# Second product of the experts on plain float32 operands, in a one-core kernel of attention, experts and a gated linear unit

## The chip, the core and the metric

The program runs on one core of one Trainium2 chip. The metric is the device time of one execution in microseconds (us); the time before is the median of three runs. TensorE (PE in the profile) does the matrix products, with its weight loads in a row of their own (PEld); VectorE is DVE, ScalarE is ACT, GpSimd is POOL, SyncE is SP and issues most transfers. The profile is one execution recorded by the hardware.

## The reference

Three layers follow each other over 3072 tokens of 512 numbers: banded attention, a mixture of experts, and a gated linear unit.

```python
x = attn_out.transpose(0, 2, 1, 3).reshape(B * S, H * D)     # 3072 x 512
x = _moe_ref(x=x, **moe_kwargs)
return _moe2_ref(x=x, **moe2_kwargs)
# _moe_ref: do_compute = x @ w_skip > 0; e_idx = argmax(x[do_compute] @ w_gate)
for e in range(E):                                           # E = 8
    mask = e_idx == e
    h = np.maximum(xc[mask] @ w1[e], 0.0)                    # 512 -> 1024
    y[mask] = gate_w[mask, None] * (h @ w2[e])               # 1024 -> 512
out[do_compute] = xc + y
# _moe2_ref: gate = 1/(1+exp(-(x @ w_gate))); (gate * (x @ w_val)) @ w_out, 512 -> 1536 -> 512
```

The weights of the gated linear unit arrive as float64 and are converted on the chip.

## The kernel before

The attention comes first (to about 290 us), then the experts (to about 556 us), then the gated linear unit. Most products are made in three parts: each operand is split into a high part of type float32r (ScalarE copies it, which rounds) and a low part, the difference (VectorE or GpSimd subtracts), and TensorE adds up high times high, high times low and low times high. A few products run on plain float32 operands: probabilities times values in the attention (L413, L414, 65 columns wide). Transposes (L443, L762) take plain float32 too.

The experts' weights come in chunks of 512 KB, numbered n: for expert e, 8e to 8e+3 are w1 and 8e+4 to 8e+7 are w2. `load_chunk` brings a chunk into a ring of six raw buffers; `split_chunk` makes the two parts (L733 on ScalarE, L735 on VectorE or GpSimd). GpSimd takes the low parts of the chunks with n % 8 in (0, 2, 6) and of the first ones, VectorE the others. Expert 0 is done as two tiles of 128 tokens ("0a", "0b") by `expert_tile`, in the wait for the routing of the last batch; experts 1 to 7 are done by `expert`, each with 256 places for tokens; a further tile of 128 tokens ("overflow", e = 8), which runs with these inputs, is done by `expert_tile` at the end.

In `expert` the first product (L779) has 96 matmuls of 256 columns; its result is relu'd and split into `hT` (L783, L784). The second product (L801) has 16 products of 512 columns, three matmuls each. `hook1` follows each quarter of the first product and `hook2` each quarter of the second; between them they put into the queues, in program order, the splits of the next expert's chunks, the transposes of the next expert's tokens (L762, L765, L766), the gather of the tokens of the expert after that (L748) and the steps of `convert` for the gated linear unit's weights: words loaded into `cvw` by SP (L1173), squares on ScalarE (L1182), L1195, L1196, L1199 and then L1201, L1202 on VectorE, and an addition on GpSimd (L1203). Each engine works through its queue in that order. SP's queue holds the chunk loads and the `cvw` loads in program order as well, and a load whose buffer is still in use holds up those behind it.

Of the kernel before, what the change touches and what calls it, by code (L numbers as in the profile page):

```python
# [63 lines left out]
def attention_moe_glu_kernel(  # L64
# [14 lines left out]
    # ------------------------------------------------------------------ constants  # L79
# [40 lines left out]
    # expert weights: quads of four [128, 1024] chunks, w1(0), w2(0), w1(1), ...  # L120
# [14 lines left out]
    def load_chunk(n, after=None):  # L135
        t = (raw_p if n % 6 > 3 else rawb[0]).tile([P, 1024], F32, tag="raw", name=f"raw{n}")
        src = chunk_src(n)
        if after is not None:
            after.memset(t[:, 0:1], 0.0)
        nc.sync.dma_start(t if (n % 8) < 4 else t.rearrange("p (a f) -> p a f", a=2), src)  # L140
        raw_q[n] = t

    chunks = {}
    general = []

    # ------------------------------------------------------------------ attention
    with ExitStack() as actx:
# [14 lines left out]
        # distances, and a large number for what is masked: the scores of head h are taken times 2^(h+1), the  # L162
        # reciprocal of its slope
# [31 lines left out]
        def prime_v(G):  # L195
            """value blocks 1..4 with the first keys, the global ones, in place of their own first rows"""
# [25 lines left out]
        def k_task(G, pr, c):  # L222
            """key transposes of blocks 2c, 2c+1 of a pair of heads, each stacked twice"""
# [88 lines left out]
        def prep_tasks(G):  # L312
            """(early part, late part)"""
# [33 lines left out]
        def emit_global(n):  # L347
            """the first keys, the global ones, in place of the first of the block"""
# [173 lines left out]
        # bias tiles from the run-time n_local and n_global  # L522
# [34 lines left out]
        # products of no use while the loads are under way: the array's clock goes up with its load  # L557
# [6 lines left out]
        def busy(n):  # L564
            # the same through the waits of the last logits
# [150 lines left out]
    # ------------------------------------------------------------------ experts  # L716
    with ExitStack() as ectx:
# [922 lines left out]
```

## Time and profile before

| what | value |
|---|---|
| median of three runs | 1160.47 us (1160.18 to 1168.36) |
| profiled execution: its time, the span from first to last instruction | 1162.3 us |
| TensorE busy in the span | 1080.8 us (93%) |
| VectorE, ScalarE, GpSimd busy | 775.5, 529.4, 345.7 us |
| mean granted TensorE clock | 0.960 |

The page lists one execution; its span is all the time that it gives, and it lies 1.8 us over the median. Busy shares are means over stages with different limits, so the stages have to be read apart: the page cuts the span into 40 slices, and VectorE's digits are 7 to 9 up to slice 20 and 3 or 4 from slice 25 on, where TensorE's are all 9.

### The profile page before, as it was taken

The page shows a single profiled execution, that of the slowest core. Times are in us where ns is not written, and L with a number is a line of the kernel's source. Part 1 is how long each engine was busy: PE and PEld are TensorE (multiplying, and loading weights), DVE is VectorE, ACT ScalarE, POOL GpSimd, SP SyncE. Part 2 cuts the span into 40 slices and gives each one's busy share as a digit, 9 for nine tenths or more (in the row PEclk, how much of TensorE's full clock was granted, in tenths as well). Part 3 has the DMA queues.
Part 4 walks back from the last instruction along what each step waited for, and adds up shares of the span by engine and source line. Part 5 has one row for each costly group of instructions (what it writes and reads, how often), then busy time and mean ns, then how long its engine had stood idle before and what let it go on. Part 6 is the DMA issues. An engine that isn't in the chain of part 4 may idle for free.

```text
span 1162.3 us, 16223 instructions
## 1 busy us (share of the span) xinstructions
PE 1080.8 (93%) x5870; PEld 927.1 (80%) x5870; DVE 775.5 (67%) x1584; ACT 529.4 (46%) x929; POOL 345.7 (30%) x349
## 2 busy tenths in 40 slices
PE   6899899898888888888999999999999999999998
PEld 6788888887677777776787888888888888888886
DVE  6899879797679999998788734443444343444342
ACT  5787666665334444445444433333433333333232
POOL 3786565673546556554222100000000000000000
PEclk7999888899899988889999999999999999999999
DMA  8355455252457777765332110020010002001000
GB/s 164 100 146 137 102 124 132 65 148 80 150 188 252 237 234 231 232 229 171 100 109 73 37 55 1 1 73 1 1 60 14 1 1 73 1 1 37 1 1 36
DMA packets 104106, 110.23 MB, mean 95 GB/s; under 512 B 55888, under 2 KB 82256, under 8 KB 103632
## 3 DMA queue, kind: packets, MB, share of 16 engines
q1 hardware_dynamic: 101296, 100.18, 29.3%
q0 software_dynamic: 2720, 8.92, 2.1%
q8 instruction: 49, 0.80, 0.3%
q14 instruction: 41, 0.34, 0.1%
HBM read 86.27 MB, written 17.30 MB: 89 GB/s over the span
## 4 chain that ended last, share of the span: by engine, by line
PE 48%; DVE 3%; issue 0%; ACT 0%; DVEq 0%
PE gv L1080 32%; PE o L1100 16%; PE gx L1046 1%; DVE wgvs L1057 0%; DVE wgv L1196 0%; DVE wo L1199 0%; DVE wo L1196 0%; DVE gt L1088 0%; DVE gm L1086 0%; ACT gt L1087 0%; DVE cvbo L1202 0%; DVE wos L1064 0%; DVE gxl L1040 0%; DVE cvbo L1201 0%; PE gx L1035 0%
## 5 line engine op out<-in xcount | busy, mean ns | idle before, releaser
L1080 PE MATMUL gv<-gxh,wgvs 128*128 128x512 f32 x1152 | 367.7, 391 | 1.7 <-ACT gxh L1039 1.0
L1080 PEld LDWEIGHTS gv<-gxh,wgvs 128*128 128x128 f32 x1152 | 216.1, 188 | 46.9 <-ACT gxh L1039 1.2
L1080 PE MATMUL gv<-gxl,wgvs 128*128 128x512 f32 x576 | 223.4, 389 | 0.3 <-DVE gxl L1040 0.3
L1100 PE MATMUL o<-wos,gt 128*128 128x512 f32 x864 | 207.6, 389 | 0.0
L1086 DVE TENSOR_TENSOR gm<-gv,sg 128x512 f32<-128x512 f32 x72 | 49.7, 690 | 221.4 <-PE gv L1080 221.4
L1100 PEld LDWEIGHTS o<-wos,gt 128*128 128x128 f32 x864 | 162.1, 188 | 33.9 <-DVE wos L1064 0.3
L1087 ACT ACTIVATE gt<-gm 128x512 fp32r<-128x512 f32 x72 | 45.5, 632 | 216.2 <-DVE gm L1086 216.2
L1080 PEld LDWEIGHTS gv<-gxl,wgvs 128*128 128x128 f32 x576 | 108.2, 188 | 22.6 <-DVE gxl L1040 0.7
L779 PE MATMUL h<-xeh,we 128*128 128x256 f32 x448 | 93.6, 308 | 24.2 <-POOL we L735 18.0
L376 ACT ACTIVATE p<-t,mn 128x256 f32<-128x256 f32 (+1 forms) x192 | 83.3, 482 | 63.8 <-DVE mn L367 63.5
L1085 ACT ACTIVATE sg<-gv 128x512 f32<-128x512 f32 x72 | 43.0, 598 | 135.1 <-PE gv L1080 122.1
L779 PEld LDWEIGHTS h<-xeh,we 128*128 128x128 f32 x448 | 78.4, 213 | 27.2 <-POOL we L735 19.0
L1057 DVE TENSOR_TENSOR wgvs<-wgv,wgvs 128x1024 fp32r<-128x1024 f32 x72 | 91.0, 1264 | 11.1 <-ACT wgvs L1056 10.9
L1088 DVE TENSOR_TENSOR gt<-gm,gt 128x512 fp32r<-128x512 f32 x72 | 49.9, 693 | 50.2 <-ACT gt L1087 50.2
L801 PE MATMUL y<-we,hT 128*128 128x512 f32 x336 | 81.8, 395 | 1.7 <-DVE we L735 1.7
L342 PE MATMUL s<-ks,qs 128*128 128x256 f32 (+1 forms) x384 | 72.8, 313 | 9.3 <-DVE ks L352 5.1
L367 DVE CUSTOM_DVE_ANT_0 t<-s,far 128x256 f32<-128x256 f32 (+1 forms) x192 | 68.7, 394 | 15.1 <-PE s L342 14.6
L1056 ACT ACTIVATE wgvs<-wgv 128x1024 fp32r<-128x1024 f32 x72 | 75.5, 1049 | 0.4 <-ACTq L1558 0.4
L735 POOL TENSOR_TENSOR we<-raw,we 128x1024 fp32r<-128x1024 f32 (+1 forms) x27 | 67.9, 2522 | 25.6 <-ACT we L733 13.5
L733 ACT ACTIVATE we<-raw 128x1024 fp32r<-128x1024 f32 x68 | 70.6, 1052 | 9.7 <-DMA raw<-in_moe_w_dram 6.2
L414 PE MATMUL o<-v,pts 128*128 128x65 f32 x384 | 73.3, 284 | 0.4 <-PE pt L385 0.4
L801 PEld LDWEIGHTS y<-we,hT 128*128 128x128 f32 x336 | 61.5, 188 | 14.2 <-DVE we L735 2.1
(268 smaller groups left out, 1856.8 us busy)
## 6 DMA issues: line engine op xcount, KB each, us to landing
raw<-in_moe_w_dram SPq DMA_DIRECT2D x68, 512.0 KB, 4.1
qraw<-in_q_dram SPq DMA_DIRECT2D x16, 384.0 KB, 3.6
kraw<-in_k_dram SPq DMA_DIRECT2D x32, 192.0 KB, 4.0
v<-in_v_dram SPq DMA_DIRECT2D x8, 768.0 KB, 5.6
x_rows<-x SPq DMA_DIRECT2D x48, 128.0 KB, 2.4
cvwg<-in_moe_w_gate_dram SPq DMA_DIRECT2D x12, 512.0 KB, 4.9
cvwg<-in_moe_w_val_dram SPq DMA_DIRECT2D x12, 512.0 KB, 4.9
cvwo<-in_moe_w_out_dram SPq DMA_DIRECT2D x12, 512.0 KB, 3.5
```

The costliest lines, as they stand in the source:

```text
L342: nc.tensor.matmul(st[:, a, c0:256], qt[:, a, i * P:(i + 1) * P], kt[:, a, e, k0:(i + 1) * P], start=(e == 0), stop=(e == 1))
L367: nc.vector.tensor_tensor_reduce(o, i0, i1, 2.0 ** -(h0 + a + 1), 3.0e38, ALU.add, ALU.min, mn[:, a:a + 1])
L376: nc.scalar.activation(p[:, a, c0:], t[:, a, c0:], AF.Exp, bias=mn[:, a:a + 1], scale=-1.0)
L414: nc.tensor.matmul(o[:, hh, :], t[:, a, 1, :], vt[:, hh, i, :], start=(i == 0), stop=True)
L733: nc.scalar.activation(t[:, 0, :], r, AF.Copy)
L735: low = lambda sl: eng.tensor_tensor(t[:, 1, sl], r[:, sl], t[:, 0, sl].bitcast(F32), ALU.subtract)
L779: nc.tensor.matmul(ph[:, a, :n], chunks[cb + c][:, wl, m * P:(m + 1) * P], xx[:, c, :n], start=(s_ == 0), stop=(s_ == len(seq) - 1))
L801: nc.tensor.matmul(ys[u], hh[:, hl, f % 2, u * P:(u + 1) * P], w[:, wl, (f % 2) * DM:(f % 2 + 1) * DM], start=(f == 0 and s_ == 0), stop=( ...
L1056: nc.scalar.activation(t[:, 0], wgv[m], AF.Copy)
L1057: nc.vector.tensor_tensor(t[:, 1], wgv[m], t[:, 0].bitcast(F32), ALU.subtract)
L1080: nc.tensor.matmul(pt, w[:, wl, c, gv, :], xx[:, c, :], start=(i == 0), stop=(i == len(seq) - 1))
L1100: nc.tensor.matmul(ops[g][u], gt[:, hl, u * P:(u + 1) * P], w[:, wl, :], start=(m == 0 and i == 0), stop=(m == NM - 1 and i == 2))
```

## The change

The second product of every expert takes plain float32 operands: the relu'd first product is kept once as float32, and the w2 chunks are used as they are loaded, so that one matmul instruction stands where three stood. The low part of `hT` and both parts of the w2 chunks are no longer made. The w1 chunks are still split, all their low parts now on VectorE. The w2 chunks have eight buffers of their own ("web", of 4 KB per partition where four of 8 KB were); the ring of six raw buffers holds w1 chunks, and chunks 4 and 5 at the start. Loads go out as buffers come free by count (`free`, `loads`) and not by the count of splits. The four splits per expert are all issued from `hook2`.

```diff
     def load_chunk(n, after=None):
-        t = (raw_p if n % 6 > 3 else rawb[0]).tile([P, 1024], F32, tag="raw", name=f"raw{n}")
+        if n % 8 > 3:
+            pool, tag = (raw_p, "raw") if n < 6 else (web[0], "web")
+        else:
+            pool, tag = (raw_p if ring_place(n) > 3 else rawb[0]), "raw"
+        t = pool.tile([P, 1024], F32, tag=tag, name=f"raw{n}")
...
-        web = ectx.enter_context(tc.tile_pool(name="web", bufs=4))
+        web.append(ectx.enter_context(tc.tile_pool(name="web", bufs=8)))
...
-        def split_chunk(n, late=None):
-            pool, tag = (wea, "wea") if n % 8 < 4 else (web, "web")
-            t = pool.tile([P, 2, 1024], F32R, tag=tag, name=f"we{n}")
+        def split_chunk(n):
+            t = wea.tile([P, 2, 1024], F32R, tag="wea", name=f"we{n}")
             r = raw_q.pop(n)
             nc.scalar.activation(t[:, 0, :], r, AF.Copy)
-            eng = nc.gpsimd if n < 6 or n == 9 or n % 8 in (0, 2, 6) and n < 8 * NE + 1 else nc.vector
...
+            nc.vector.tensor_tensor(t[:, 1, :], r, t[:, 0, :].bitcast(F32), ALU.subtract)
...
-                hh = hp.tile([P, 2, 2, 2 * P], F32R, tag="h", name=f"hT{key}_{mp}")
-                nc.scalar.activation(hh[:, 0, :, :n], ph[:, :, :n], AF.Relu)
-                nc.vector.scalar_tensor_tensor(
-                    hh[:, 1, :, :n], ph[:, :, :n], 0.0, hh[:, 0, :, :n].bitcast(F32), ALU.max, ALU.subtract)
+                hh = hp.tile([P, 2, 2 * P], F32, tag="h", name=f"hT{key}_{mp}")
+                nc.scalar.activation(hh[:, :, :n], ph[:, :, :n], AF.Relu)
...
-                for s_, (hl, wl) in enumerate(((0, 0), (0, 1), (1, 0))):
-                    nc.tensor.matmul(
-                        ys[u], hh[:, hl, f % 2, u * P:(u + 1) * P],
-                        w[:, wl, (f % 2) * DM:(f % 2 + 1) * DM],
-                        start=(f == 0 and s_ == 0), stop=(f == NF - 1 and s_ == 2))
+                nc.tensor.matmul(ys[u], hh[:, f % 2, u * P:(u + 1) * P], w[:, (f % 2) * DM:(f % 2 + 1) * DM],
+                                 start=(f == 0), stop=(f == NF - 1))
+                if f % 2 == 1 and u == nt - 1:
+                    used[0] += 1
...
+        def free(n):
+            k = n // 8 * 4 + n % 4
+            if n % 8 > 3:
+                return k < 10 or used[0] > k - 8
+            return k < 8 or (used[0] > k - 8 if k < 10 else nsplit[0] > k - 6)
+
+        def loads():
+            while nload[0] < 8 * NE + 8 and not hold[0] and free(nload[0]):
+                load_chunk(nload[0])
+                nload[0] += 1
...
             def hook1(mp, e=e):
-                split_next()
...
             def hook2(fq, e=e):
                 if fq == 1 and e + 2 <= NE:
                     gather(e + 2, cols(idx, e + 2))
+                split_next()
                 if fq < 2:
-                    split_next()
                     prep_x(e + 1, 2 if e + 1 < NE else 1, fq)
-                if fq in (1, 2):
-                    split_next()
+                loads()
```

`expert_tile` changes in the same way (in place of three matmuls per product one; its two copies of `hT` go to ScalarE and VectorE in turn, and VectorE subtracts nothing), and the splits of chunks 4 to 7 that `at_a` issued during the routing are gone. Line numbers move: L779 becomes L784, L801 becomes L803, L735 becomes L745, L748 becomes L753, L795 becomes L798 and L140 becomes L145.

TensorE's queue in expert 1, at the end of the first product and in the first half of the second. Before (`we` holds split chunks, `hT` the split relu'd rows, `y_0` and `y_1` are the sums of the two tiles of tokens, `xe` the next expert's transposes):

```order
L779 MATMUL h_3_7166<-xeh_6917,we_6991 128x256
L801 MATMUL y_0_7205<-we_7059,hT_0_7056 128x512 x3
L801 MATMUL y_1_7206<-we_7059,hT_0_7056 128x512 x3
L801 MATMUL y_0_7205<-we_7059,hT_0_7056 128x512 x3
L801 MATMUL y_1_7206<-we_7059,hT_0_7056 128x512 x3
L762 MATMUL xe_0_7226<-ident,xg_7011 128x128 x4
L801 MATMUL y_0_7205<-we_7093,hT_1_7090 128x512 x3
```

The same place in the changed kernel (`raw` is a chunk as loaded):

```order
L784 MATMUL h_3_7113<-xeh_6888,we_6954 128x256
L803 MATMUL y_0_7146<-raw_6803,hT_0_7021 128x512
L803 MATMUL y_1_7147<-raw_6803,hT_0_7021 128x512
L803 MATMUL y_0_7146<-raw_6803,hT_0_7021 128x512
L803 MATMUL y_1_7147<-raw_6803,hT_0_7021 128x512
L767 MATMUL xe_0_7159<-ident,xg_6966 128x128 x4
L803 MATMUL y_0_7146<-raw_6805,hT_1_7049 128x512
```

Three instructions became one, on the loaded chunk; the transposes keep their place.

GpSimd's queue from the results of expert 1 to those of expert 2. Before (`xg` are gathered rows, `cvbg` and `wgv` belong to the conversion, `xo` are results scattered to the rows):

```order
L795 DMA x_rows<-xo_1_7330,idx 3200x512
L735 TENSOR_TENSOR we_7435<-raw_7251,we_7435 128x1024
L1203 TENSOR_TENSOR wgv_6668<-wgv_6668,cvbg_7403 128x4x128
L735 TENSOR_TENSOR we_7498<-raw_7283,we_7498 128x1024
L1203 TENSOR_TENSOR wgv_6668<-wgv_6668,cvbg_7480 128x4x128
L748 DMA xg_7527<-x_rows,idx 128x512 x2
L735 TENSOR_TENSOR we_7542<-raw_7397,we_7542 128x1024
L1203 TENSOR_TENSOR wgv_6669<-wgv_6669,cvbg_7551 128x4x128
L795 DMA x_rows<-xo_0_7595,idx 3200x512
```

The same stretch in the changed kernel:

```order
L798 DMA x_rows<-xo_1_7247,idx 3200x512
L1203 TENSOR_TENSOR wgv_6668<-wgv_6668,cvbg_7308 128x4x128
L1203 TENSOR_TENSOR wgv_6668<-wgv_6668,cvbg_7373 128x4x128
L753 DMA xg_7404<-x_rows,idx 128x512 x2
L1203 TENSOR_TENSOR wgv_6669<-wgv_6669,cvbg_7427 128x4x128
L798 DMA x_rows<-xo_0_7464,idx 3200x512
```

The three subtractions per expert are gone; the additions, gathers and scatters keep their order.

SP's queue in experts 1 and 2. Before (`cvwg` are the words of the conversion, 512 KB like a chunk):

```order
L140 DMA raw_7364<-in_moe_w_dram 128x1024
L140 DMA raw_7397<-in_moe_w_dram 128x1024
L1173 DMA cvwg_7401<-in_moe_w_val_dram 128x4x256
L140 DMA raw_7438<-in_moe_w_dram 128x1024
L140 DMA raw_7474<-in_moe_w_dram 128x2x512
L1173 DMA cvwg_7478<-in_moe_w_gate_dram 128x4x256
```

In the changed kernel, over the second product of expert 1:

```order
L145 DMA raw_7155<-in_moe_w_dram 128x1024
L145 DMA raw_7176<-in_moe_w_dram 128x1024
L145 DMA raw_7178<-in_moe_w_dram 128x2x512
L145 DMA raw_7180<-in_moe_w_dram 128x2x512
L145 DMA raw_7199<-in_moe_w_dram 128x2x512
L1173 DMA cvwg_7203<-in_moe_w_gate_dram 128x4x256
```

Here five chunks stand together ahead of the words, three of them w2 chunks (128x2x512) whose buffers come free when TensorE has used the chunk eight places earlier.

## Rows read from the trace of the kernel before

**Rows 1.** Busy time by stretch (us from the span's start), granted clock, DMA share:

```profile
core 0: us, PE busy (x) PEld busy (x) DVE busy (x) ACT busy (x) POOL busy (x), PEclk, DMA share, GB/s
331.80:538.50 206.70, 180.51 (x1085) 162.26 (x1084) 193.29 (x210) 93.46 (x123) 116.51 (x66) 0.93 0.68 221
391.00:422.00 31.00, 27.10 (x157) 24.13 (x158) 29.79 (x31) 12.97 (x17) 18.50 (x12) 0.89 0.75 234
700.00:1162.00 462.00, 458.20 (x2051) 378.79 (x2049) 191.35 (x245) 161.37 (x244) 0.00 (x0) 1.00 0.05 19
```

**Rows 2.** Timeline of TensorE, expert 1 (start us, us, operation, count):

```profile
331.82 0.28 PE L779 MATMUL h<-xeh,we 128*128 128x256 f32 x1
337.57 2.77 PE L1408 MATMUL rB<-scr,scr 128*128 128x72 f32 x24
...
346.00 2.91 PE L801 MATMUL y<-we,hT 128*128 128x512 f32 x12
...
352.32 5.72 PE L801 MATMUL y<-we,hT 128*128 128x512 f32 x24
357.88 0.28 PE L779 MATMUL h<-xeh,we 128*128 128x256 f32 x1
```

**Rows 3.** Timeline of TensorE, first product of expert 3:

```profile
385.89 0.28 PE L779 MATMUL h<-xel,we 128*128 128x256 f32 x1
391.22 0.80 PE L779 MATMUL h<-xeh,we 128*128 128x256 f32 x2 [5.05 <-POOL we L735]
```

**Rows 4.** Timeline of GpSimd, the same stretch:

```profile
386.17 0.99 POOL L748 DMA_INDIRECT xg<-x_rows,idx  x1
...
388.69 2.48 POOL L735 TENSOR_TENSOR we<-raw,we 128x1024 fp32r<-128x1024 f32 x1
```

**Rows 5.** Waits from 300 to 560 us (total, times, longest):

```profile
PE h L779 <- POOL we L735: 18.0, 5, 5.1
...
ACT cvcg L1182 <- DMA cvwg<-in_moe_w_val_dram: 10.3, 2, 6.4
```

**Rows 6.** Groups of VectorE, experts 3 and 4 (391.2 to 452.6 us):

```profile
L735 DVE TENSOR_TENSOR we<-raw,we 128x1024 fp32r<-128x1024 f32 x10 | 12.9, 1290 | 0.5 <-ACT we L733 0.5
L1201 DVE TENSOR_SCALAR cvbg<-wgv 128x512 int32<-128x512 int32 x8 | 11.8, 1480 | 0.1
...
L1195 DVE TENSOR_SCALAR wgv<-cvwg 128x512 int32<-128x512 int32 x8 | 8.6, 1072 | 0.0
...
L784 DVE SCALAR_TENSOR_TENSOR hT<-h,hT 128x512 fp32r<-128x512 f32 x8 | 5.5, 684 | 0.4 <-ACT hT L783 0.4
```

**Rows 7.** Conversion instructions alone, whole run (ns min/median/max):

```profile
L1195 DVE TENSOR_SCALAR wgv<-cvwg x24: 414/1030/2623, 352.2 to 626.5; 128x512 int32<-128x512 int32 x24
L1201 DVE TENSOR_SCALAR cvbg<-wgv x24: 410/424/2987, 358.9 to 629.5; 128x512 int32<-128x512 int32 x24
```

**Rows 8.** Timeline of TensorE in attention, two products on plain float32:

```profile
202.64 0.39 PE L414 MATMUL o<-v,pts 128*128 128x65 f32 x2
202.87 0.39 PE L413 MATMUL o<-v,pts 128*128 128x65 f32 x2
```

**Rows 9.** The same, 48 columns of float32r:

```profile
277.62 0.83 PE L1338 MATMUL rpx<-rt_R,rB 128*128 128x48 f32 x6
```

**Rows 10.** Durations by line (ns min/median/max):

```profile
L414 PE MATMUL o<-v,pts x384: 222/275/422, 36.6 to 283.4; 128*128 128x65 f32 x192
L443 PE MATMUL xT<-ident,x x96: 272/273/329, 51.7 to 285.3; 128*128 128x128 f32 x96
L801 PE MATMUL y<-we,hT x336: 387/389/496, 346.0 to 538.3; 128*128 128x512 f32 x168
```

**Rows 11.** Waits of TensorE from 284 to 333 us:

```profile
PE y0b L847 <- DVE hT0b L840: 2.8, 1, 2.8
...
PE rA L1338 <- DVE scr L1305: 1.5, 1, 1.5
```

**Rows 12.** Timeline of TensorE, the overflow tile's second product:

```profile
548.03 6.90 PE L847 MATMUL y<-we,hT 128*128 128x512 f32 x22 [2.01 <-DVE hT L840]
```

More of the change, by code (lines that the diff above doesn't have):

```diff
@@ L140, in load_chunk, with ring_place @@
         nc.sync.dma_start(t if (n % 8) < 4 else t.rearrange("p (a f) -> p a f", a=2), src)
-        raw_q[n] = t
+        if n % 8 > 3:
+            chunks[n] = t
+        else:
+            raw_q[n] = t
+    def ring_place(n):
+        return (n // 8 * 4 + n % 8 - 4) % 6
+    web = []
     chunks = {}
@@ L845, in expert_tile @@
                 w, hh = chunks[cb + 4 + f // 2], hs[f // 2]
-                for s_, (hl, wl) in enumerate(((0, 0), (0, 1), (1, 0))):
-                    nc.tensor.matmul(y, hh[:, hl, f % 2, :P], w[:, wl, (f % 2) * DM:(f % 2 + 1) * DM],
-                                     start=(f == 0 and s_ == 0), stop=(f == NF - 1 and s_ == 2))
+                nc.tensor.matmul(y, hh[:, f % 2, :P], w[:, (f % 2) * DM:(f % 2 + 1) * DM],
+                                 start=(f == 0), stop=(f == NF - 1))
+                if f % 2 == 1 and key != "0a":
+                    used[0] += 1
                 if f % 2 == 1:
@@ L860, in conv_load, with split_next @@
                 cvw[n] = load_words(nc, cvp, f"g{n}", gv_src(n))
-        nload = [4]
-        nsplit = [4]
-        hold = [False]
-        def loads_to(n):
-            while nload[0] < min(n, 8 * NE + 8) and not hold[0]:
+        nload, nsplit, used = [6], [4], [0]
+        hold = [True]
+        def free(n):
+            k = n // 8 * 4 + n % 4
+            if n % 8 > 3:
+                return k < 10 or used[0] > k - 8
+            return k < 8 or (used[0] > k - 8 if k < 10 else nsplit[0] > k - 6)
+        def loads():
+            while nload[0] < 8 * NE + 8 and not hold[0] and free(nload[0]):
                 load_chunk(nload[0])
                 nload[0] += 1
-        def split_next(late=None):
-            if nsplit[0] < 8 * NE + 8:
-                split_chunk(nsplit[0], late)
+        def split_next():
+            k = nsplit[0]
+            if k < 4 * NE + 4:
+                split_chunk(k // 4 * 8 + k % 4)
                 nsplit[0] += 1
-                loads_to(nsplit[0] + 5)
+                loads()
         def conv_steps():
@@ L915, in at_a @@
                 run(rt.ranks(B - 1, pr, Bm))
-                split_next(late)
                 run(rt.weights(B - 1))
@@ L921, in at_a @@
                 gather("0b", [col(idx, NE)])
-                late.pop()()
                 gather(1, cols(idx, 1))
@@ L947, in at_b @@
                 gather(2, cols(idx, 2))
+            if what[0] == "out":
+                loads()
         expert_tile("0a", 0, pcol0, col(idx, 0), at_a)
@@ L992, in attention_moe_glu_kernel @@
         with tc.If(ovr["n"] > 0):
-            def at_o(what):
-                if what in (("product", 1), ("product", 2), ("product", 3), ("product", 4)):
-                    split_next()
-            expert_tile(NE, 8 * NE, col(prob_s, NS_), col(idx, NS_), at_o)
+            expert_tile(NE, 8 * NE, col(prob_s, NS_), col(idx, NS_), lambda what: None)
     more_overflow(tc, nc, ident, w1, w2, X, idx, prob_s, ovi, ovr["n"], load_x0)
```

22 lines of the change are left out of this document (7 added, 15 removed).

## The prediction

> **What bounds the kernel now.** I read the busy times by stretch first. From 700 us to the end TensorE is busy for 458 of 462 us [rows 1]: there the gated linear unit is bound by TensorE, so a microsecond saved ahead of it arrives at the end. The change touches only the experts. From 331.8 to 538.5 us, experts 1 to 7, TensorE is busy for 180.5 of 206.7 us at a granted clock of 0.93, and VectorE for 193.3; in the stretch of one expert, 391 to 422 us, VectorE has 29.8 of 31.0 us [rows 1]. VectorE is the bound here, and TensorE waits for what stands behind it.
>
> The timeline of expert 1, which runs without a stop, says what TensorE alone needs. The first product takes from 331.82 to 346.00 us, of which the 24 routing products at L1408 take some 2.6; that leaves 11.6. The second product takes from 346.00 to 357.88, or 11.9 us, with 0.232 us per matmul (24 in 5.56 us) and some 0.7 us of transposes [rows 2]. So an expert needs 11.6 + 11.9 = 23.5 us, seven need 164.3, with the routing products 166.9. The stretch takes 206.7: **39.8 us are waiting and slow clock.** The timeline of expert 3 shows how: after the seventh matmul TensorE stands idle for 5.05 us, until GpSimd has made a low part of a w1 chunk [rows 3]; GpSimd starts that part at 388.69, behind its gathers [rows 4], which stand in its queue behind an addition that needs VectorE. The list of waits puts 18.0 us on this line in five waits [rows 5]. After the idle time the clock is lower: 0.89 over expert 3's stretch [rows 1], which at levels of 1.2 and 2.4 GHz is some 7 us of 31 at the lower one.
>
> **The change part by part.**
>
> *TensorE's work.* Per expert, 48 float32r matmuls of 512 columns become 16 plain ones. How a plain product runs is seen in the attention: it is recorded as two MATMULs, and a pair of 65 columns starts 0.23 us after the pair ahead of it [rows 8], 0.115 us per record. That is no price per column: six float32r matmuls of 48 columns take 0.83 us together [rows 9], less the last one's own 0.27 or so, 0.112 us from start to start; something other than the columns sets this pace. So the record of 512 columns is bounded. It can't be cheaper than a float32r matmul of that width, 0.232 us; and if the 0.115 us did grow with the columns, it would be 0.91 us. The durations decide where between: the shortest 65-column plain record takes 222 ns, a 128-column transpose on plain float32 takes 272, so 0.79 ns per further column; float32r takes 0.28 us at 256 columns [rows 2] and 0.389 at 512 [rows 10], 0.43 ns per column. A plain column costs some 1.85 times as much. 512 x 0.79 ns is 0.41 us, and float32r's pitch lies some 10 to 20 ns over 512 x 0.43; I take **0.44 us per record**, an estimate from these rows, nearest to twice the float32r price. A product then costs 0.88 us where three matmuls cost 0.70. Second product: 32 x 0.44 = 14.1 us in place of 11.1; an expert needs 11.6 + 0.7 + 14.1 = 26.4 us, seven and the routing products 187.4.
>
> The Trainium skill's page "FP8 and Floating Point Precision", section "TensorE Precision Notes", speaks against the change: true FP32 takes four passes through the array (H*H + H*L + L*H + L*L). Four passes at the 0.232 us of a float32r matmul make 0.93 us a product, 0.05 more than mine, and the sum below would end some 7 us later.
>
> *VectorE's work.* The low part of `hT` goes: eight of 0.684 us in two experts, 2.7 us per expert. One of five w1 or w2 low parts goes, 1.3 us [rows 6]. GpSimd's three low parts per expert go from GpSimd. These cost VectorE more than they show: the conversion's L1195 and L1201 take 0.414 and 0.410 us at best but up to 2.6 and 3.0 [rows 7], and in experts 3 and 4 they take 1.07 and 1.48 on average [rows 6], which I put down to GpSimd's work beside them. If that excess goes with the low parts, four each per expert give 4 x 0.66 + 4 x 1.07 = 6.9 us. VectorE is left with 29.8 - 2.7 - 1.3 - 6.9 = 18.9 us per expert; if GpSimd's additions, which stay, hold it up as much as before, with 25.8. Both are under TensorE's 26.4. The four low parts of w1 now stand in the second product, 4 x 1.29 of its 14.1 us, ahead of the next first product.
>
> **So TensorE becomes the bound,** and 206.7 becomes 187.4 us: -19.3. No idle time of 5 us is left ahead of a first product, so I expect the clock to stay up too, which is in this number.
>
> *Loads.* In SP's queue up to five chunks now stand ahead of a word load, w2 chunks among them that wait until TensorE has used the chunk eight places earlier. Who waits for a late word load is ScalarE at L1182, with the relu of the next first product behind it, and so TensorE. Such waits of ScalarE exist already, 10.3 us in two, the longest 6.4 [rows 5], and cost TensorE nothing while it is waiting anyway; without that cover each could cost from nothing to 6.4. A whole expert of prefetch stands against it, and the DMA share of 0.68 over 206.7 us [rows 1] becomes 0.75. I add 1.5 us, for experts 1 and 2, where the deeper prefetch is being filled.
>
> *The three single tiles.* Each second product becomes 16 x 0.44 = 7.0 in place of 24 x 0.232 = 5.6 us: +1.4, three times 4.3. In exchange VectorE no longer subtracts in `hT`, for which TensorE waits 2.8 us in tile 0b [rows 11] and 2.0 in the overflow tile [rows 12], and the wait for the one-hot rows, 1.5 us [rows 11], ends earlier, since GpSimd's low parts are out of the routing. -6.3 + 4.3 = -2.0.
>
> Sum: 1162.3 - 19.3 + 1.5 - 2.0 = 1142.5 us against the profiled execution; that lies 1.8 over the median, so against 1160.5 I say **1141 us**.
>
> **The rivals.**
>
> *The wait moves.* Word loads, the splits packed into one product, or GpSimd's additions keep half of the distance between 26.4 us and today's 206.7 / 7 = 29.5: seven times 1.55, 11 us more, 1152. For it: VectorE's upper bound of 25.8 leaves 0.6 us of room, and all its w1 work now has to be done in 14 us. Against it: the lower bound of 18.9, and a prefetch that is an expert deep.
>
> *The plain record is as cheap as float32r's,* 0.232 us. TensorE needs 11.6 + 0.7 + 7.4 = 19.7 us per expert and is no longer the bound; VectorE with 18.9 to 25.8 is, and the transfers, 0.68 x 29.5 = 20 us of full share. At 24 us per expert the stretch takes 171; the single tiles save 6 more: about 1119. The durations speak against it. The Trainium skill's "Perfetto Trace Analysis", section "Engine Utilization", halves the output rate for FP32_LOW_HIGH; if that is the rate of the whole product, it is this case; rows 8 show two records, so a half rate per record, which is mine, reads as well.
>
> *Slower: the plain record is dearer.* If its time grows as the pitch of the 65-column records does, it takes 0.91 us. There are 7 x 32 + 3 x 16 = 272 records; +0.47 each are 128 us, 1269. It decides from the point where the 19.5 us saved are spent: 19.5 / 272 = 0.07, so from 0.51 us per record. For it: no row shows a plain product of 512 columns. Against it: the 48-column float32r row at the same pitch, and the shortest 222 ns. A clock that goes down to the lower level in the second products would be the same price, 0.88; but the granted clock is mostly full in the attention, with its many plain products.
>
> **How the numbers follow.** About 1% (12 us) is what a measurement of this kernel can tell from no change: faster ends at 1149. Chances: forecast 0.58 (1132 to 1149; the two ends are 0.42 and 0.46 us per record, 272 x 0.02 = 5 us each way, and waits of 0 to 5 us); the wait that moves 0.18 (1146 to 1160, a third of it under 1149); cheap record 0.08 (1112 to 1130); slower 0.10; nothing gained, since expert by expert a new wait eats it, 0.06. The range 1124 to 1158 takes in the forecast, most of the second case and half of the third, some 0.8. Faster 0.58 + 0.06 + 0.08, and a share of the moved wait that ends just under the bound, 0.75; same 0.15; slower 0.10.
>
> **What would show it.** In the profile of the changed kernel, the second product's groups (L803 in `expert`) should hold two records per product with starts 0.44 us apart, the stretch of experts 1 to 7 some 187 us at a clock near 1.00, TensorE without the idle times at the first product, L1195 and L1201 near 0.42 us, and VectorE's share of the stretch near 70%. The prediction is wrong if the record's pitch is under 0.3 or over 0.5 us, if TensorE waits for ScalarE's relu behind L1182, or if the clock drops inside the second product.

## The result, and the profile after

The changed kernel takes **1135.6 us** (median of four runs, 1134.1 to 1136.2) against 1160.4 for the kernel before on the same chip (four runs): a ratio of 0.976, 95% interval 0.9735 to 0.9784, faster. The forecast was 1141, range 1124 to 1158. The profiled execution's span is 1134.3 us, 28.0 under that of before. One execution of experiment 1 took 5649 us and is left out of its median, since the other nine lie between 1156 and 1168.

Busy time by stretch of the changed kernel: experts 1 to 7, experts 3 and 4 in it, and expert 0's two tiles ahead of them.

```profile
core 0: us, PE busy (x) PEld busy (x) DVE busy (x) ACT busy (x) POOL busy (x), PEclk, DMA share, GB/s
327.30:512.30 185.00, 185.00 (x973) 130.73 (x972) 120.36 (x174) 63.72 (x92) 64.95 (x47) 1.00 0.72 252
382.20:434.40 52.20, 52.20 (x273) 36.69 (x272) 36.86 (x52) 18.64 (x27) 21.31 (x16) 1.00 0.79 273
293.98:327.30 33.32, 32.94 (x125) 21.61 (x125) 22.38 (x64) 9.65 (x17) 11.23 (x14) 0.92 0.69 235
```

Against [rows 1] the stretch of experts 1 to 7 went from 206.7 to 185.1 us, and the bound changed hands: TensorE is busy for all of it, at a granted clock of 1.00; VectorE fell from 193.3 to 120.4, 18.4 per expert in experts 3 and 4. The other parts: expert 0's tiles 39.5 to 33.3 us, the overflow tile with the start of the next layer 17.5 to 15.4, and the attention ends 1.6 us later; this differs from run to run: in experiments 1 and 2, with the code of before up to there, it ends 5 us earlier than before. -21.6 - 6.2 - 2.1 + 1.6 is -28.3, against -28.0 for the span.

Timeline of TensorE, end of expert 1's first product, its second product, and the first matmul of expert 2 (start us, us, operation, count):

```profile
341.74 0.28 PE L784 MATMUL h<-xeh,we 128*128 128x256 f32 x1
341.86 3.60 PE L803 MATMUL y<-raw,hT 128*128 128x512 f32 x8
345.29 0.60 PE L767 MATMUL xe<-ident,xg 128*128 128x128 f32 x4
345.73 3.60 PE L803 MATMUL y<-raw,hT 128*128 128x512 f32 x8
349.17 0.60 PE L767 MATMUL xe<-ident,xg 128*128 128x128 f32 x4
349.60 7.03 PE L803 MATMUL y<-raw,hT 128*128 128x512 f32 x16
356.07 0.68 PE L784 MATMUL h<-xeh,we 128*128 128x256 f32 x1
```

This answers to [rows 2]. Thirty-two records stand there for 16 products, two each; eight of them take from 341.86 to 345.29, so **0.429 us from start to start** and 0.858 per product, where three float32r matmuls took 0.70. The second product takes 14.2 us in place of 11.9, and the next expert starts behind it without a gap (at such a change of line the profile's modelled durations overlap). Each of experts 2 to 6 takes 26.12 us.

Durations of single instructions over the whole run (ns min/median/max): the plain records, and the conversion on VectorE that answers to [rows 7].

```profile
L803 PE MATMUL y<-raw,hT x224: 590/592/595, 341.9 to 512.3; 128*128 128x512 f32 x112
L1195 DVE TENSOR_SCALAR wgv<-cvwg x24: 405/427/1490, 338.1 to 598.1; 128x512 int32<-128x512 int32 x24
L1201 DVE TENSOR_SCALAR cvbg<-wgv x24: 416/421/428, 351.0 to 601.1; 128x512 int32<-128x512 int32 x24
```

The conversion instructions, up to 2.6 and 3.0 us before, now mostly take their least time. All waits of TensorE from 300 to 530 us, which answers to [rows 5] (us in total, times, longest):

```profile
PE gx L1035 <- DVEq L1558: 1.1, 1, 1.1
PE ht0b L837 <- ACT hr0b L832: 0.3, 1, 0.3
```

None is left in experts 1 to 7. The waits of the other engines from 284 to 545 us show who has time now:

```profile
DVE wgv L1195 <- DMA cvwg<-in_moe_w_val_dram: 12.7, 7, 2.6
ACT cvcg L1182 <- DMA cvwg<-in_moe_w_val_dram: 12.1, 2, 6.1
DVE wgv L1195 <- DMA cvwg<-in_moe_w_gate_dram: 6.9, 4, 2.5
```

VectorE waits for transfers, the sign that it has room. ScalarE's longest wait for words is as long as before (6.1 us, 6.4 before), and still nobody on TensorE waits behind it.

### The profile page after: what moved, and what is told of

Read it like the earlier page. It is cut to its first block, busy times and chain, and to the rows that moved or that the text cites. A ratio compares the mean times of both kernels' runs of the same rounds, so it can differ in the third digit from the quotient of the medians.

```text
span 1134.3 us, 15800 instructions
## 1 busy us (share of the span) xinstructions
PE 1087.6 (96%) x5734; PEld 890.1 (78%) x5734; DVE 687.7 (61%) x1540; ACT 491.7 (43%) x887; POOL 278.4 (25%) x322
## 4 chain that ended last, share of the span: by engine, by line
PE 49%; DVE 3%; issue 0%; ACT 0%; DVEq 0%
PE gv L1080 33%; PE o L1100 16%; PE gx L1046 1%; DVE wgvs L1057 0%; DVE wgv L1196 0%; DVE gm L1086 0%; DVE gt L1088 0%; ACT gt L1087 0%; DVE wos L1064 0%; DVE wo L1199 0%; DVE wo L1196 0%; DVE cvbo L1202 0%; DVE gxl L1040 0%; PE gx L1035 0%; DVE cvbo L1201 0%
## 5 line engine op out<-in xcount | busy, mean ns | idle before, releaser
L803 PE MATMUL y<-raw,hT 128*128 128x512 f32 x224 | 99.6, 592 | 0.0
L784 PE MATMUL h<-xeh,we 128*128 128x256 f32 x448 | 84.7, 289 | 0.0
L803 PEld LDWEIGHTS y<-raw,hT 128*128 128x128 f32 x224 | 41.0, 190 | 43.6 <-issue 43.3
L784 PEld LDWEIGHTS h<-xeh,we 128*128 128x128 f32 x448 | 70.3, 192 | 1.7 <-issue 1.7
L311 POOL TENSOR_TENSOR qs<-qr,qs 64x384 fp32r<-64x384 f32 x56 | 58.9, 1052 | 34.9 <-DVE qs L310 31.6
L354 PEld LDWEIGHTS s<-ks,qs 128*128 128x128 f32 x384 | 56.7, 204 | 13.1 <-DVE ks L364 7.7
```

Source lines behind the costliest of these rows:

```text
L311: nc.gpsimd.tensor_tensor(dst[hi_, s], qr[lo_], dst[lo_, s].bitcast(F32), ALU.subtract)
L354: nc.tensor.matmul(st[:, a, c0:256], qt[:, a, i * P:(i + 1) * P], kt[:, a, e, k0:(i + 1) * P], start=(e == 0), stop=(e == 1))
L784: nc.tensor.matmul(ph[:, a, :n], chunks[cb + c][:, wl, m * P:(m + 1) * P], xx[:, c, :n], start=(s_ == 0), stop=(s_ == len(seq) - 1))
L803: nc.tensor.matmul(ys[u], hh[:, f % 2, u * P:(u + 1) * P], w[:, (f % 2) * DM:(f % 2 + 1) * DM], start=(f == 0), stop=(f == NF - 1))
```

## The experiments

All times are medians, ratios are to the kernel before on the same chip (1160 to 1167 us there). A trace shows one execution; those of experiments 1 and 3 lie 7 and 5 us under the medians. The first theory is the prediction's: VectorE was the bound, above all through what GpSimd's low parts add to it; freed of that, TensorE sets the pace at the price of its plain products. The main rival is that the cheaper or shorter second product itself brings the time.

**1. Only the products plain** (kernel before, experts 1 to 7; the low parts are still made, and nobody reads those of the second product).

```diff
-                for s_, (hl, wl) in enumerate(((0, 0), (0, 1), (1, 0))):
-                    nc.tensor.matmul(
-                        ys[u], hh[:, hl, f % 2, u * P:(u + 1) * P],
-                        w[:, wl, (f % 2) * DM:(f % 2 + 1) * DM],
-                        start=(f == 0 and s_ == 0), stop=(f == NF - 1 and s_ == 2))
+                nc.tensor.matmul(
+                    ys[u], hh[:, 0, f % 2, u * P:(u + 1) * P].bitcast(F32),
+                    w[:, 0, (f % 2) * DM:(f % 2 + 1) * DM].bitcast(F32),
+                    start=(f == 0), stop=(f == NF - 1))
```

> The kernel before, with the second product of experts 1 to 7 as one plain float32 matmul on the high parts in place of three; the low parts are still made, but this leaves them out of the sum. TensorE's work is then the changed kernel's, all else is as before. Theory (VectorE is the bound before, the gain is VectorE's relief): VectorE's 29.5 us per expert stay, so no gain, 1155 to 1170 us. Rival (the plain products bring the gain by themselves, by fewer instructions or a steadier clock): 1136 to 1145 us.

Measured: 1163.2, ratio 0.999 [0.997, 1.001]. Experts 1 to 7 in this kernel:

```profile
327.50:531.70 204.20, 190.65 (x974) 134.19 (x972) 192.68 (x210) 92.81 (x123) 113.30 (x66) 0.98 0.70 224
```

VectorE is busy for 192.7 of 204.2 us, as before. One expert of seven reached 26.12 us, the others took 28.4 to 30.6. Plain products by themselves bring nothing.

**2. Less work for TensorE still** (kernel before; the second product of experts 1 to 7 takes high times high only).

```diff
-                for s_, (hl, wl) in enumerate(((0, 0), (0, 1), (1, 0))):
...
+                nc.tensor.matmul(
+                    ys[u], hh[:, 0, f % 2, u * P:(u + 1) * P],
+                    w[:, 0, (f % 2) * DM:(f % 2 + 1) * DM],
+                    start=(f == 0), stop=(f == NF - 1))
```

> The kernel before, with only the high-times-high float32r matmul of the three in the second product of experts 1 to 7; the two others are left out of the sum, their operands are still made. TensorE needs 11.1 x 2/3 = 7.4 us less per expert, 16 in place of 23.5. Theory: VectorE is the bound, so little comes of it, 1145 to 1160 us. Rival (TensorE's work bounds the experts): 7 x 7.4 = 52 us less, some 1108 us.

Measured: 1165.0, ratio 1.0005 [0.9986, 1.0024]. I had allowed for a small gain; there is none. Experts 1 to 7, the overflow tile with the start of the next layer behind them, and TensorE's two longest lists of waits in the experts:

```profile
328.10:525.80 197.70, 139.79 (x862) 126.64 (x860) 184.06 (x201) 87.03 (x117) 110.46 (x64) 0.80 0.69 223
525.80:552.10 26.30, 17.64 (x58) 12.28 (x56) 20.18 (x24) 10.37 (x15) 8.89 (x5) 0.81 0.40 126
```

```profile
PE h L779 <- POOL we L735: 23.4, 7, 5.1
PE h L779 <- DVE xel L766: 22.1, 6, 4.7
```

TensorE has 32 matmuls less per expert, some 52 us in all at 0.232 each, and is busy for 41 us less; the rest went into a clock of 0.80 (0.93 before). The saved time became waits. Experts 1 to 7 are 9 us shorter, but the stretch behind them takes 26.3 in place of 17.5 us, so nothing is left of it. Over both stretches VectorE is busy for as long as before: 184.1 + 20.2 us here, 193.3 + 11.5 there. So VectorE's work set the time, and TensorE was not the bound of these experts.

**3. Only the low parts moved** (kernel before; products in three parts, all low parts on VectorE).

```diff
-            eng = nc.gpsimd if n < 6 or n == 9 or n % 8 in (0, 2, 6) and n < 8 * NE + 1 else nc.vector
+            eng = nc.vector
```

> The kernel before, with all low parts of chunks on VectorE, none on GpSimd; three-part products as before. VectorE takes 3 x 1.22 = 3.7 us more per expert. Theory with the hold-up of VectorE by GpSimd as large as forecast (6.9 us per expert): 3.2 us less per expert, 1138 to 1150 us. Rival (the hold-up is small, VectorE's plain amount of work counts): 3.7 us more per expert, 1175 to 1187 us.

Measured: **1136.7, ratio 0.977 [0.974, 0.980]: as large a gain as that of the whole change, by one line.** The gain is larger than I expected (1138 to 1150), since I left out expert 0's tiles (34.0 us here, 39.5 before). Experts 1 to 7, and all waits of TensorE there:

```profile
322.20:508.80 186.60, 170.59 (x1086) 153.44 (x1085) 176.26 (x233) 93.01 (x123) 64.65 (x47) 0.99 0.76 247
```

```profile
PE h L779 <- DVE we L735: 8.7, 6, 1.8
PE h L779 <- DVE hT L784: 5.8, 5, 1.4
PE y L801 <- DVE we L735: 1.5, 1, 1.5
```

VectorE has 21 low parts more to make and is busy for 17 us less. The groups of VectorE in experts 1 to 7 (busy us, mean ns | idle before) tell where that is from. The kernel before:

```profile
L735 DVE TENSOR_TENSOR we<-raw,we 128x1024 fp32r<-128x1024 f32 x35 | 50.1, 1431 | 1.6 <-ACT we L733 1.6
L1195 DVE TENSOR_SCALAR wgv<-cvwg 128x512 int32<-128x512 int32 x22 | 26.8, 1217 | 0.0
L1196 DVE SCALAR_TENSOR_TENSOR wgv<-cvwg,wgv 128x512 int32<-128x512 int32 x22 | 26.5, 1203 | 0.8
L1201 DVE TENSOR_SCALAR cvbg<-wgv 128x512 int32<-128x512 int32 x21 | 23.3, 1112 | 0.2
```

With all low parts on VectorE:

```profile
L735 DVE TENSOR_TENSOR we<-raw,we 128x1024 fp32r<-128x1024 f32 x56 | 74.6, 1334 | 1.3 <-ACT we L733 1.3
L1196 DVE SCALAR_TENSOR_TENSOR wgv<-cvwg,wgv 128x512 int32<-128x512 int32 x22 | 18.2, 825 | 0.8
L1195 DVE TENSOR_SCALAR wgv<-cvwg 128x512 int32<-128x512 int32 x22 | 14.6, 663 | 0.0
L1201 DVE TENSOR_SCALAR cvbg<-wgv 128x512 int32<-128x512 int32 x21 | 8.8, 421 | 0.2
```

The low parts cost 24.5 us more; these three conversion groups alone give back 35.0 (76.6 to 41.6), 5.0 us per expert. Over all its instructions it is 43 us, 6.1 per expert: 21 more low parts of 1.22 us are 25.6, and VectorE is busy for 17.0 less. The whole trace of before says the same: of VectorE's 209 instructions in experts 1 to 7, 37 took over 0.1 us longer than the shortest of their line and shape, 55 us together, and every one of the 37 overlaps an instruction of GpSimd, 27 of them (46.5 us) a low part. One pair of instructions of the kernel before shows how. GpSimd's low part of [rows 4] runs from 388.69 to 391.17. VectorE, same stretch:

```profile
388.88 2.57 DVE L1201 TENSOR_SCALAR cvbg<-wgv 128x512 int32<-128x512 int32 x1
```

It starts 0.19 us behind GpSimd's and ends at 391.45, 0.28 us after GpSimd's has ended, where it takes 0.42 alone. The Trainium skill's page "SBUF — State Buffer", section "Who interferes with whom", says that VectorE and GpSimd share one pair of ports as an exclusive lock, which VectorE needs in a two-port mode (which a `tensor_scalar` like this one can take) or with two operands in SBUF, and that the second to issue blocks until the first has finished; the trace agrees with it here, with 2.57 us in place of 0.42.

**4. Work of GpSimd that nobody waits for.** The theory so far leaves a rival: the price might have been TensorE's waits for GpSimd's late low parts [rows 3, 5], not the slower VectorE. So the kernel of experiment 3, and the changed kernel, get three differences per expert on GpSimd, of high parts with themselves, which nobody reads, in eight pieces each; the diff is that of the kernel of experiment 3, and in the changed one, where only w1 chunks are split, (0, 2, 3) stands for (0, 2, 6).

```diff
             chunks[n] = t
+            if n >= 10 and n % 8 in (0, 2, 6) and n < 8 * NE:
+                g = ep.tile([P, 128], F32R, tag="unread", name=f"unread{n}", bufs=1)
+                for k in range(8):
+                    hi = t[:, 0, k * 128:(k + 1) * 128].bitcast(F32)
+                    nc.gpsimd.tensor_tensor(g, hi, hi, ALU.subtract)
```

> The kernel before with all low parts on VectorE (e3), and in experts 1 to 7 GpSimd makes three differences per expert of 128 x 1024 elements that nobody reads, each in eight pieces of 128 columns. Theory (GpSimd's subtractions slow VectorE's conversion instructions while they run beside them, and that was the price of having them there): VectorE, 25.2 us per expert in e3, gets some 5.6 us on top, the gain is gone, and more than that, since the three low parts that VectorE makes stay: stretch of experts 1 to 7 at 205 us or more, time 1155 to 1180. Rival (the price was TensorE's waits for low parts that GpSimd finished late): nothing waits for the unread pieces, stretch 187 us, time 1137 within 5.

> The changed kernel with the same three unread differences per expert on GpSimd, after the splits of the w1 chunks 0, 2 and 3. Theory (TensorE is the bound and VectorE has room): VectorE goes from 17.2 to about 23 us per expert, still under TensorE's 26.1; time 1136 to 1143, conversion instructions up to 1.5 us and more again. Rival (there is no room to use, since VectorE's work is packed into the second product): each expert loses the 5.6 us, time 1165 to 1178.

Measured, on the kernel of experiment 3: 1163.8, ratio 1.0017 [0.9997, 1.0037]; the whole gain is gone again. Experts 1 to 7, the longest list of waits of TensorE, the pieces on GpSimd, and a group of VectorE:

```profile
325.30:534.00 208.70, 182.80 (x1085) 163.38 (x1084) 186.04 (x229) 92.92 (x122) 165.53 (x193) 0.91 0.66 220
```

```profile
PE h L784 <- DVE we L735: 22.9, 14, 3.7
```

```profile
L745 POOL TENSOR_TENSOR unread<-we 128x128 fp32r<-128x128 f32 x148 | 103.7, 701 | 16.8 <-ACT we L733 6.5
```

```profile
L1206 DVE TENSOR_SCALAR cvbg<-wgv 128x512 int32<-128x512 int32 x21 | 13.1, 624 | 10.1 <-POOL wgv L1208 10.0
```

TensorE waits for no low part of GpSimd here, and yet 22 us are lost in the stretch (186.6 to 208.7): the rival alone doesn't carry it. But the price came by two ways: VectorE's busy time grew by 9.8 us, less than the 5.6 per expert that I expected, since it now stands beside short pieces (L1206 here, L1201 in experiment 3: 624 ns on average in place of 421), and VectorE waited 10.0 us for an addition that stood behind the pieces in GpSimd's queue. Eight pieces take 5.6 us where one low part took 2.7, so GpSimd is at 165.5 us and late itself, which it was less in the kernel before (116.5). How much of the price in the kernel before was hold-up and how much lateness is thus not measured apart. For the lateness speak the 18.0 us that TensorE waited for GpSimd's low parts [rows 5], out of 26.2 us of idle time; for the hold-up, that VectorE was busy for 193 of 207 us there, and that it lost 46.5 us beside these low parts. The two are linked, since GpSimd itself waited 44.6 us there for VectorE, at the addition that stands ahead of the low parts in its queue.

On the changed kernel: 1143.4, ratio 0.984 [0.982, 0.986], at the upper end of what I expected and far from the rival's 1165. VectorE goes to 139.2 us and is still not the bound; the stretch grows by 6.3 us, 4.0 of it in this wait of TensorE:

```profile
PE h L789 <- DVE we L745: 4.0, 3, 2.0
```

So the same work on GpSimd costs some 27 us where VectorE is the bound and some 8 where TensorE is, by the medians.

**5. Room in the changed kernel.** Three kernels put something back, one thing each. Low parts of the w1 chunks 0 and 2 of experts 2 to 7 on GpSimd:

```diff
-            nc.vector.tensor_tensor(t[:, 1, :], r, t[:, 0, :].bitcast(F32), ALU.subtract)
+            eng = nc.gpsimd if n % 8 in (0, 2) and 10 < n < 8 * NE else nc.vector
+            eng.tensor_tensor(t[:, 1, :], r, t[:, 0, :].bitcast(F32), ALU.subtract)
```

> The changed kernel, with the low parts of w1 chunks 0 and 2 of experts 2 to 7 back on GpSimd. VectorE does 2.4 us less per expert and is held up by up to 2 x 2.4. Theory (TensorE is the bound now, VectorE has 18.4 of 26.1 us, so room): no difference, 1134 to 1140 us. Rival (the hold-up itself costs time wherever it stands, or the first product waits for GpSimd again): 1143 us or more.

Measured: 1137.2, ratio 0.978 [0.974, 0.981]. The stretch is 4.5 us longer, in two or three experts, and TensorE waits again, for VectorE:

```profile
323.09:512.63 189.54, 185.84 (x974) 130.93 (x973) 120.77 (x162) 64.12 (x92) 89.56 (x59) 1.00 0.70 246
PE h L785 <- DVE we L746: 3.7, 3, 1.9
```

VectorE makes twelve low parts less in this stretch (15 in place of 27, 14.6 us at 1.22) and is busy for as long, 120.8 us against 120.4. What it was spared came back as longer instructions: here, without TensorE waiting for GpSimd, the hold-up stands by itself.

The low part of `hT` made, and not read:

```diff
+                lo = hp.tile([P, 2, 2 * P], F32, tag="lo", name=f"lo{key}_{mp}", bufs=2)
+                nc.vector.scalar_tensor_tensor(
+                    lo[:, :, :n], ph[:, :, :n], 0.0, hh[:, :, :n], ALU.max, ALU.subtract)
```

> The changed kernel, with VectorE making the low part of hT again in experts 1 to 7 (nobody reads it), 2.7 us more per expert on VectorE. Theory (VectorE has 18.4 of 26.1 us per expert, so room): no difference to the changed kernel, 1133 to 1139 us. Rival (each microsecond off VectorE is gained, on it lost): 7 x 2.7 = 19 us more, some 1155 us.

Measured: 1136.9, ratio 0.976 [0.971, 0.980]; 19 us more work on VectorE make the stretch 3.6 us longer. Four buffers for w2 in place of eight:

```diff
-        web.append(ectx.enter_context(tc.tile_pool(name="web", bufs=8)))
+        web.append(ectx.enter_context(tc.tile_pool(name="web", bufs=4)))
...
-                return k < 10 or used[0] > k - 8
+                return k < 6 or used[0] > k - 4
```

> The changed kernel with four buffers for w2 chunks in place of eight, so that their loads go out half an expert later. Theory (the loads play no part in the gain): no difference, 1133 to 1139 us. Rival (the deeper prefetch holds the new bound): waits of TensorE on w2 chunks or of ScalarE on word loads, 1142 us or more.

Measured: 1137.6, ratio 0.976 [0.973, 0.980], stretch 3.5 us longer. None of the three is more than 2 us from the changed kernel in its time. So none of the three parts was needed for the gain by itself, and that holds for the moved low parts of w1 too: in the kernel before, moving the low parts was enough (experiment 3); in the changed kernel, with two of the three per expert back on GpSimd and the third no longer made, the plain products and the work that they spare VectorE reach the same height. All three put back at once was not run.

**6. Where part of the gain lies ahead of the experts** (kernel before; only the low parts of chunks 4 to 11, of which GpSimd makes six during the routing and expert 0's tiles, on VectorE).

```diff
-            eng = nc.gpsimd if n < 6 or n == 9 or n % 8 in (0, 2, 6) and n < 8 * NE + 1 else nc.vector
+            eng = nc.gpsimd if n >= 12 and n % 8 in (0, 2, 6) and n < 8 * NE + 1 else nc.vector
```

> The kernel before, with only the first eight chunks' low parts (those made during the routing and the two tiles of expert 0) on VectorE; from chunk 12 on GpSimd has its share as before. Theory (GpSimd's low parts hold up VectorE wherever they stand, so the routing and the tiles of expert 0 gain by themselves): tiles 0a and 0b take some 34 us in place of 39.5, experts 1 to 7 their 29.5 each, some 1155 us against 1160. Rival (all of the gain is in experts 1 to 7, the tiles gain by the plain product or the loads): no difference to the kernel before.

Measured: 1160.9, ratio 0.997 [0.995, 0.9997]; expert 0's tiles take 34.5 in place of 39.5 us, experts 1 to 7 are no shorter (208.4, 206.7 before). Timeline of VectorE in the routing of the last batch, the kernel before and then this one:

```profile
293.18 2.47 DVE L1258 TENSOR_TENSOR rt_E<-rt_key,rt_sm 128x48 f32<-128x48 f32 x1
...
296.23 1.77 DVE L1263 TENSOR_TENSOR_SCAN rt_I<-rt_ones,rt_E 128x48 f32<-128x48 f32 x1
298.04 1.12 DVE L1265 TENSOR_TENSOR rt_bip<-rt_cnt,rt_I 128x7 f32<-128x7 f32 x1
```

```profile
295.20 0.25 DVE L1258 TENSOR_TENSOR rt_E<-rt_key,rt_sm 128x48 f32<-128x48 f32 x1
...
295.67 0.25 DVE L1263 TENSOR_TENSOR_SCAN rt_I<-rt_ones,rt_E 128x48 f32<-128x48 f32 x1
295.95 0.17 DVE L1265 TENSOR_TENSOR rt_bip<-rt_cnt,rt_I 128x7 f32<-128x7 f32 x1
```

Three small instructions took 4.7 us longer beside GpSimd's low parts. The tiles are 5 us shorter by that edit alone, in the trace. Of the time 3 us are measured, with an interval from 0.3 to 6, so the time alone hardly tells it from no change.

**7. Is TensorE now the bound, and by how much?** The changed kernel with every second plain product left out in experts 1 to 7:

```diff
-                nc.tensor.matmul(ys[u], hh[:, f % 2, u * P:(u + 1) * P], w[:, (f % 2) * DM:(f % 2 + 1) * DM],
-                                 start=(f == 0), stop=(f == NF - 1))
+                if f % 2 == 1:
+                    nc.tensor.matmul(ys[u], hh[:, f % 2, u * P:(u + 1) * P], w[:, (f % 2) * DM:(f % 2 + 1) * DM],
+                                     start=(f == 1), stop=(f == NF - 1))
```

> The changed kernel with every second plain product of the second product left out in experts 1 to 7 (8 of 16), so TensorE needs 26.1 - 6.9 = 19.2 us per expert; VectorE's 18.4 stay. This asks what comes next behind TensorE. Theory: VectorE and the transfers (0.72 of the 26.4 us at full share, 19 us) come next, at 21 to 24 us per expert, so 15 to 36 us less than the changed kernel, 1100 to 1121 us. Rival (VectorE's room is not usable, since its work stands in the second product, which is now 7 us): 25 us per expert or more, 1128 us or more.

Measured: 1123.4, ratio 0.964 [0.959, 0.969], over the 1100 to 1121 that I expected and under the rival's 1128. Experts 1 to 7 and the wait of TensorE:

```profile
328.00:503.80 175.80, 150.49 (x845) 119.69 (x844) 127.23 (x175) 63.16 (x91) 65.26 (x47) 0.91 0.73 255
```

```profile
PE h L784 <- DVE we L745: 25.2, 12, 3.5
```

48 us of products left out (112 x 0.429) make the stretch 9 us shorter. VectorE's 127 us of 176 are not the bound as a sum, but its low parts of w1 all have their place in the second product, among waits for words; when that product is half as long, they come late, TensorE waits 25 us and the clock falls to 0.91. So the rival has the cause right, though not the size: VectorE's room can't be used freely.

**8. A mixture of both.** Since TensorE is the bound and VectorE has some 8 us per expert left, the last one, or the last two, of an expert's four w2 chunks are split again and their products done in three float32r matmuls (w2 buffers 6 and 4, for room). `H2` is (3,) or (2, 3), and `w2s` holds the parts of those chunks; their splits, left out of the diff, are issued in the first product of the same expert, where no low part of w1 stands.

```diff
+                if mp in H2:
+                    hh = hp.tile([P, 2, 2, 2 * P], F32R, tag="h2", name=f"hT{key}_{mp}", bufs=1)
+                    nc.scalar.activation(hh[:, 0, :, :n], ph[:, :, :n], AF.Relu)
+                    nc.vector.scalar_tensor_tensor(
+                        hh[:, 1, :, :n], ph[:, :, :n], 0.0, hh[:, 0, :, :n].bitcast(F32), ALU.max, ALU.subtract)
...
+                if f // 2 in H2:
+                    w = w2s[f // 2]
+                    for s_, (hl, wl) in enumerate(((0, 0), (0, 1), (1, 0))):
+                        nc.tensor.matmul(ys[u], hh[:, hl, f % 2, u * P:(u + 1) * P],
+                                         w[:, wl, (f % 2) * DM:(f % 2 + 1) * DM],
+                                         start=(f == 0 and s_ == 0), stop=(f == NF - 1 and s_ == 2))
```

> The changed kernel, with the last of the four w2 chunks of experts 1 to 7 split again and its products in three float32r matmuls (six buffers for w2). TensorE does 4 x (0.858 - 0.681) = 0.7 us less per expert, VectorE 1.9 us more. Theory (TensorE is the bound, VectorE has room): 5 us less than the changed kernel, 1128 to 1133 us. Rival (the room is used up by where the work stands): no gain or a loss, 1135 us or more.

> The same with the last two w2 chunks split (four buffers for w2). TensorE does 1.4 us less per expert, 24.7 us, VectorE 3.8 more, 22.2 us. Theory: 10 us less than the changed kernel, 1122 to 1128 us, if VectorE's work fits in where it stands. Rival: VectorE becomes the bound again, no better than with one chunk.

Measured: one chunk 1130.2, ratio 0.9695 [0.966, 0.973]; two chunks 1128.7, ratio 0.9685 [0.965, 0.972]. Both beat the changed kernel, by 5 and 7 us; the second just misses what I expected. Experts 1 to 7 with two chunks, and the wait of TensorE:

```profile
326.20:506.10 179.90, 176.86 (x1031) 141.59 (x1030) 150.68 (x202) 77.39 (x106) 66.53 (x47) 1.00 0.76 268
```

```profile
PE h L786 <- DVE we L747: 3.0, 3, 1.2
```

TensorE still leads with 176.9 of 179.9 us; the first waits for VectorE are back. Between the two the measurement tells no difference.

## Why the prediction was right

*What bounds.* Right: some 52 us less of matmuls in experiment 2 brought nothing, while VectorE relieved of one cause in experiment 3 brought as much as the whole change. The waits of TensorE and its low clock followed from VectorE's lateness, in part by way of GpSimd, whose queue waits for VectorE, as read from [rows 1 to 5]; how much by either way is not measured apart.

*TensorE's work.* Right: the record was put at 0.44 us and took 0.429, the expert at 26.4 and took 26.12, the stretch at 187.4 and took 185.1. The working's own terms (512 x 0.79 ns, which is 0.40 and not 0.41, and 10 to 20 ns) make 0.41 to 0.42; it took 0.44, and the measurement lies between. The ratio that the working took from the 65- and 128-column durations, 1.85 times float32r, is what came out: 0.429 / 0.232 = 1.85. The rivals on the record (0.232 and 0.91) fall. The Trainium skill's four passes, from "FP8 and Floating Point Precision", section "TensorE Precision Notes", would make 0.93 us a product; the trace has 0.858, 8% under that, so they hold roughly, with the product recorded as two instructions.

*VectorE's work.* Right: 18.9 us per expert forecast, 18.4 measured in experts 3 and 4. The term of 6.9 us that I put down to GpSimd's low parts is there: experiment 3 shows 5.0 of it in three groups and 6.1 over all of VectorE, and its cause is seen in the 37 long instructions of the kernel before, all beside GpSimd, and in the low parts put back in experiment 5. How much of the time of before came by it, and how much by TensorE's waits for GpSimd, experiment 4 leaves open.

*The clock.* Right: granted 1.00, 0.93 before.

*The loads.* The +1.5 us did not come: TensorE has no wait in experts 1 to 7, and with half of the w2 buffers it takes 2 us more.

*The single tiles.* Here the step failed in size: -2.0 forecast, -8.3 measured (-6.2 and -2.1). Expert 0's tiles and the overflow tile before, a wait of TensorE in tile 0b that [rows 11] leaves out, and the overflow tile in the changed kernel:

```profile
292.37:331.80 39.43, 33.12 (x140) 26.32 (x141) 29.78 (x66) 14.57 (x25) 26.45 (x21) 0.87 0.60 203
538.50:556.00 17.50, 14.40 (x58) 10.69 (x57) 11.50 (x15) 5.29 (x9) 3.21 (x3) 0.90 0.38 122
PE ht0b L835 <- ACT hr0b L830: 1.9, 1, 1.9
512.30:527.70 15.40, 14.34 (x50) 8.31 (x49) 4.60 (x8) 3.02 (x5) 2.99 (x2) 1.00 0.26 87
```

The term that was wrong is the price of the dearer products, +4.3 us. TensorE's busy time didn't grow at all, 33.1 to 32.9 us in expert 0's tiles and 14.4 to 14.3 in the overflow tile, while the granted clock there rose from 0.87 to 0.92 and from 0.90 to 1.00: the float32r products of before had not run at the clock that their price of 0.232 us assumes (22 of them took 6.90 us in [rows 12]). The waits that I counted, 6.3 us, are gone, and with them most of the 1.9 at `ht0b` (0.3 is left), which I did not count. Together that is 8.2 of the 8.3 us; experiment 6 puts 5.0 of the 6.2 in expert 0's tiles on GpSimd's low parts alone.

*The sum.* That 1141 came within 6 us of 1135.6 is in part luck. The profiled executions have to be compared by their spans, and there the forecast is 1142.5 against 1134.3, 8.2 too long: 6.3 by the tiles, 3.8 by experts 1 to 7 with the loads (188.9 against 185.1), less 1.6 by the attention. Taking off 1.8 us to come to the median was also wrong, since a time on record is some 1.7 us longer than its span: the profiled execution before lay some 3.5 us over the median.

*The rivals.* The wait that moves did not: VectorE's 17 to 18 us were far from its upper bound of 25.8. But experiments 4, 5 and 7 show that the reason for it was sound: the low parts packed into the second product come late as soon as VectorE is held up more (TensorE waits 4.0 and 3.7 us for them) or that product gets shorter (25.2 us).

What the prediction didn't see is that its two parts aren't a chain. The working reads as if the plain products were needed to reach 185 us; the low parts moved off GpSimd reach 186.6 with the old products. The rest moves the bound from VectorE to TensorE at the same height. Nor is the moving needed once the products are plain: with two of the three low parts per expert back on GpSimd the changed kernel loses 2 us at most by the medians (experiment 5). The change holds two ways to the same time, and the sum of the prediction counts them as one.

## What to carry to other kernels

Before work is shared out to an idle engine, look at what it does to the busy one: here three subtractions per expert on GpSimd, 53 us of its time, cost VectorE some 43 us, more than the 25 us that VectorE needs to do them itself. Look for the sign in the profile: the same instruction on the same shape with a mean far over its minimum, ending together with an instruction of the other engine. And when a change has several parts, put each in alone and take each out alone: here one line was enough by itself and yet could nearly be spared beside the others, and the best version splits the second product between the two engines.

## What the runs showed of the hardware

A plain float32 product of 512 columns is recorded as two matmuls of 0.429 us from start to start, 590 to 595 ns each; 112 products, 224 records, within 1%. At 65 columns the records start 0.115 us apart [rows 8].

A VectorE instruction of 0.42 us took 2.57 beside a GpSimd subtraction and ended just after it, and instructions of 48 columns took 1.8 and 2.5 us in place of 0.25; VectorE's own low part of 1024 columns (1.22 us at best) is half of GpSimd's 2.43 us median. Short pieces on GpSimd, 0.55 us at the median, hold VectorE up less per instruction (at most 1.51 us for L1206 of experiment 4, where L1201 of before took up to 2.99), but eight of them take twice as long as one whole (5.6 and 2.7 us on average).

TensorE's granted clock was 1.00, its upper level, through 185 us of mixed float32r and plain float32 products without a gap. It was lower where waits stood between them: 0.91 in experiments 4 and 7 with some 25 us of waits, 0.80 in experiment 2 with 58, but 0.99 in experiment 3 with 16 us in waits of at most 1.8.
